# Layer-norm rows in two halves, with Newton roots on VectorE and the first row block loaded first

## The chip, the cores and the metric

The kernel runs on one core of one Trainium2 chip. The metric is the time of one execution on the device in microseconds (us). "Span" is the time from the first to the last instruction in a profiled execution; it is some 1.8 us shorter than the time of that same execution. Engines are named TensorE (PE in the profile, with PEld for its weight loads), VectorE (DVE), ScalarE (ACT), GpSimd (POOL) and SyncE (SP).

## The reference, cut to what matters

The result mixes two branches over the same rows x (2048 rows of 640). Branch A is a causal convolution over 2048 positions; branch B is a layer norm and an MLP that mixes positions.

```python
def _layernorm(x, axis=-1, eps=1e-5):
    m = jnp.mean(x, axis=axis, keepdims=True)
    v = jnp.var(x, axis=axis, keepdims=True)
    return (x - m) / jnp.sqrt(v + eps)

# branch A: S = 2048, D = 640
k_shift = sum over t of k_pad[:, t:t+S] * shift_k[:, 3-t]      # 4 filter taps   (paraphrased)
kv  = k_shift * v
y   = irfft(rfft(kv, 2*S) * rfft(ssm_k, 2*S))[:S] + kv * ssm_D #                 (paraphrased)
a   = q * y
# branch B: F = 1536
h = _layernorm(x, axis=-1)
u = _gelu(jnp.einsum("bsd,sf->bdf", h, w1) + b1)
b = (jnp.einsum("bdf,fs->bds", u, w2) + b2).transpose(0, 2, 1)

g = _sigmoid((x * gate_w).sum(-1, keepdims=True))              # x is also q
return g * a + (1 - g) * b
```

## The kernel before

The program builds a list of operations; a list scheduler then walks through a model of the engines (a duration and a priority for every operation) and fixes the order of instructions on each engine. So a changed duration in the model, or a changed operation, can move instructions anywhere. In the program that it hands over the order is fixed, with semaphores between the engines.

The work on TensorE is, in order: transposes of the filter `ssm_k`, two forward transforms of the filter (`wT` by the sine tables `FTB`), the tap convolution of k (`KF` by `KT`), the forward transforms of `kv` (`vkv`, `kv`), inverse transforms (by `GTB`), and in between the two MLP layers (`X` by `ring`, which holds w1; `GT` by `W`, which holds w2). MLP matmuls fill whatever holes the rest leaves, once rows of `X` are normalised.

The layer norm and the taps, before (the lines are those that the change touches):

```python
        def ln_tile(hk, p):                       # 16 row tiles of 128x640
            t = 4 * hk + p
            xs = X[:, hk, p, :]
            for ci in range(2):
                ... bn_stats(stats[:, t, 6*ci:6*ci+6], xs[:, 320*ci:320*ci+320])   # VectorE
            ... bn_aggr(mv[:, t, :], stats[:, t, :])                               # VectorE

        def ln_apply():
            ts("POOL", sd[:, :], mv[:, :, 1], 1e-5, None, ALU.add)
            tt("POOL", rstd[:, :], sd[:, :], V(cst, 1, [[0, 16]]), ALU.pow)        # power -0.5
            tt("POOL", sd[:, :], sd[:, :], rstd[:, :], ALU.mult)
            for t in range(16):
                xs = X[:, t // 4, t % 4, :]
                ts("DVE", xs, xs, mv[:, t, 0:1], rstd[:, t:t + 1], ALU.subtract, ALU.mult, ...)
        ...
                for hk in range(4):
                    for p in range(4):
                        ln_tile(hk, p)
                ln_apply()
                for g0 in (0, 10):                # filter taps spread out, two pieces of 128x2240
                    tt("POOL", KF[:, g0:g0 + 10, :, :], ..., ALU.mult)
                for hk in range(2):
                    k_turn(hk)                    # copies kp <- kn on VectorE, then a DMA transpose
                mixing(C[0], SS, 0, fine=True)    # sums and differences of the transformed filter, VectorE
```

The kv product, for which the first kv transform waits, is a VectorE operation behind all of these: `tt("DVE", o, kb[:, :, :], vi, ALU.mult, prio=0)`.

Of the kernel before, what the change touches and what calls it, by code (L numbers as in the profile page):

```python
# [11 lines left out]
I32 = mybir.dt.int32  # L12
# [296 lines left out]
class _Op:  # L309
    __slots__ = ("eng", "dur", "emit", "prio", "idx", "ndep", "succ", "vt", "vtrole", "end", "start", "kind", "lat", "deps", "name", "after", "nafter", "asucc")  # L310
# [12 lines left out]
class _Sched:  # L323
# [29 lines left out]
    def add(self, eng, dur, emit, reads, writes, prio=None, vt=None, lat=0.0, name=""):  # L353
# [4 lines left out]
        op.vt = vt  # L358
        deps = set()
# [22 lines left out]
    def run(self):  # L382
# [13 lines left out]
        free = {e: 0.0 for e in engs}  # L396
        dma_free = 0.0
# [14 lines left out]
        while started < n:  # L412
# [6 lines left out]
            for e in engs:  # L419
# [32 lines left out]
                if e in ("SP", "QA") or op.lat < 0:  # L452
                    issue = 0.1
                    s = max(t + issue, dma_free)
                    dma_free = s + op.dur
                    op.end = dma_free + 2.0 + (3.0 if e == "POOL" else 0.0)
                    free[e] = t + issue
                else:
                    op.end = t + op.dur
                    free[e] = op.end  # L460
# [44 lines left out]
def _build(nc, A_q, A_k, A_v, A_shift_k, A_ssm_k, A_ssm_D, B_x, B_w1, B_b1, B_w2, B_b2, gate_w, out):  # L505
# [10 lines left out]
    with ExitStack() as es:  # L516
# [97 lines left out]
        def tt(eng, o, a, b, op, mode=2, prio=None):  # L614
            n = n_of(o)
            d = dve_dur(n, mode) if eng == "DVE" else n / 500.0 + 0.3
            return SC.add(eng, d, lambda s: T.op(eng, lambda e: e.tensor_tensor(o, a, b, op), [a, b], [o]),  # L617
                          [a, b], [o], prio=prio, name="tt")

        def ts(eng, o, a, s1, s2, op0, op1=None, mode=1, prio=None, extra=0.0):  # L620
# [8 lines left out]
            return SC.add(eng, d, lambda s: T.op(eng, f, rr, [o]), rr, [o], prio=prio, name="ts")  # L629
# [90 lines left out]
        def k_turn(hk):  # L720
# [3 lines left out]
            SC.add("DVE", 0.75, lambda s: T.op("DVE", lambda e: e.tensor_copy(ov, iv), [i[:, :, :]], [o[:, :, :]]), [i[:, :, :]], [o[:, :, :]], prio=0, name="kperm")  # L724
# [13 lines left out]

        for hk in range(2):
            ssm_load(hk)  # L740
# [4 lines left out]
        x_load(0)  # L745
        dma(gwb[:, :], dr(gate_w, 0, [[0, 128], [1, D]]), 128 * 1280, chain=True)
        for hk in range(1, 4):
            x_load(hk)
        ssm_load(2)
        ssm_load(3)  # L750

# [3 lines left out]
        iota = lambda ap, pat, b, cm: SC.add("POOL", 0.5, lambda s: T.op("POOL", lambda e: e.iota(ap, pat, base=b, channel_multiplier=cm), [], [ap]), [], [ap])  # L755
# [20 lines left out]
        for hk in range(4):  # L776
            w1_load(0, hk)

# [43 lines left out]
        def mixing(R, Th, Ts, fine=False, conj=False):  # L822
# [26 lines left out]
        def ln_apply():  # L849
            ts("POOL", sd[:, :], mv[:, :, 1], 1e-5, None, ALU.add)  # L850
            tt("POOL", rstd[:, :], sd[:, :], V(cst, 1, [[0, 16]]), ALU.pow)
            tt("POOL", sd[:, :], sd[:, :], rstd[:, :], ALU.mult)
            for t in range(16):
                xs = X[:, t // 4, t % 4, :]
                ts("DVE", xs, xs, mv[:, t, 0:1], rstd[:, t:t + 1], ALU.subtract, ALU.mult, mode=4, extra=0.16)

        srcW = lambda h: (lambda kt, p, ci: wT[:, 2 * h + kt, p, 320 * ci:320 * ci + 320])
        for h in range(2):
# [5 lines left out]
            if h == 0:  # L864
                for hk in range(4):
                    for p in range(4):
                        ln_tile(hk, p)
                ln_apply()
                for g0 in (0, 10):
                    tt("POOL", KF[:, g0:g0 + 10, :, :], V(cw, 7 * g0, [[7, 10], [1, 7], [0, 32]]), V(m32, 0, [[0, 10], [0, 7], [1, 32]]), ALU.mult)  # L870
                for hk in range(2):
                    k_turn(hk)
                mixing(C[0], SS, 0, fine=True)
            else:
                mixing(C[1], C[0], 0, conj=True)
# [277 lines left out]
```

## Time and profile before

| | before |
|---|---|
| time, median of 3 (range) | 192.79 us (192.77 to 192.95) |
| span of the profiled execution, granted clock | 190.9 us, 1.0 |
| TensorE busy | 93% |
| chain of waits | TensorE 71%, VectorE 19% |

From the profile page of the kernel before: the head, the busy time of each engine, and the chain of work that ended last, by engine.

```profile
span 190.9 us, 3358 instructions
...
PE 177.4 (93%) x1403; PEld 130.5 (68%) x1403; DVE 170.3 (89%) x195; ACT 116.4 (61%) x187; POOL 33.0 (17%) x29
...
PE 71%; DVE 19%; DMA 4%; POOL 2%; issue 2%; SPq 0%; ACT 0%; DVEq 0%
```

TensorE is busy for most of the span, but the chain also runs through VectorE for 19% of it, so part of TensorE's time is set by VectorE. Where, the timeline shows. Its columns are: start in us, length in us, engine, line of the program, operation, output<-input, shapes, how many instructions are joined, and in brackets the idle time before it with what ended it. First TensorE before:

```profile
14.29 10.29 PE L293 MATMUL pp<-wT,FTB 128*128 128x320 bf16 x64 [0.43 <-ACT wT L655]
...
45.94 4.51 PE L293 MATMUL pp<-X,ring 128*128 128x320 bf16 x32
50.28 0.43 PE L293 MATMUL pp<-vkv,FTB 128*128 128x320 bf16 x2
51.75 3.75 PE L293 MATMUL pp<-vkv,FTB 128*128 128x320 bf16 x26 [1.04 <-DVE vkv L617]
55.34 1.25 PE L293 MATMUL pp<-X,ring 128*128 128x320 bf16 x8
...
72.09 4.01 PE L293 MATMUL pp<-kv,FTB 128*128 128x320 bf16 x28
...
83.10 34.93 PE L293 MATMUL pp<-X,ring 128*128 128x320 bf16 x256
117.87 32.76 PE L293 MATMUL pp<-GT,W 128*128 128x320 bf16 x240
...
180.02 7.77 PE L293 MATMUL pp<-GT,W 128*128 128x320 bf16 x56
```

Two matmuls of the kv transform start at 50.28, and the other 26 must wait for VectorE's product until 51.75. The group at 55.34, the MLP group right behind these 28 transform matmuls, is a good **checkpoint**: the waits for the layer norm and for the first kv product lie before it. From 117.87 the second MLP layer runs, and TensorE ends at 180.02 + 7.77 = 187.79.

VectorE before, around the root:

```profile
25.41 1.45 DVE L617 TENSOR_TENSOR C<-C 128x2560 bf16<-128x2560 bf16 x1
30.05 5.79 DVE L628 TENSOR_SCALAR X<-X,mv,rstd 128x640 bf16<-128x640 bf16 x16 [3.19 <-POOL rstd L617]
```

and GpSimd before, in the same stretch:

```profile
13.65 7.84 POOL L617 TENSOR_TENSOR KF<-cw,m 128x2240 bf16<-128x2240 bf16 x2 [5.40 <-DVE mv L847]
25.60 1.39 POOL L627 TENSOR_SCALAR sd<-mv 128x16 f32<-128x16 f32 x1 [4.11 <-DVE mv L847]
27.07 2.94 POOL L617 TENSOR_TENSOR rstd<-sd,cst 128x16 f32<-128x16 f32 x1
```

GpSimd's power on 128x16 values takes 2.94 us, and VectorE stands idle for 3.19 us until it is there. Only then, at 30.05, are rows scaled. The taps (`KF`, from 13.65 to 21.49) lie beside VectorE's row statistics, which are not slowed: one tile takes 0.85 to 0.86 us from start to start, ahead of the taps as beside them.

### The profile page before, as it was taken

To read this page: it belongs to the slowest core of one execution; us is meant where nothing else is said; L and a number is where in the kernel's file an instruction comes from. 1 tells how busy PE (TensorE), PEld (TensorE's weight loads), DVE (VectorE), ACT (ScalarE), POOL (GpSimd) and SP (SyncE) were. 2 spreads that over 40 slices of the span, in tenths; PEclk is the share of its full clock that TensorE was granted. 3 is DMA by queue.
4 is the path that set the end of the run, shared out by engine and by line. 5 is a ranking of instruction groups with operands and counts; after the bars stand their busy time and mean duration, and the time that the engine had idled before them with its cause. 6 is when DMAs were issued, how large, how long until landed. Compare 5 with 4: busy or idle time off the path is not lost.

```text
span 190.9 us, 3358 instructions
## 1 busy us (share of the span) xinstructions
PE 177.4 (93%) x1403; PEld 130.5 (68%) x1403; DVE 170.3 (89%) x195; ACT 116.4 (61%) x187; POOL 33.0 (17%) x29
## 2 busy tenths in 40 slices
PE   0749989999799999999999999999999999999993
PEld 0536555678566976767777777888888777886782
DVE  7999967999999799999999969999999958999451
ACT  4799997889599999998411221131322467516632
POOL 2619563600006300010012102250000000000000
PEclk9999999999999999999999999999999999999999
DMA  5999999993799999994368914999947903210222
GB/s 155 327 412 378 372 238 230 307 407 136 136 181 306 250 232 306 272 329 96 59 138 251 231 27 138 272 208 195 263 136 224 367 18 137 72 69 2 72 103 103
DMA packets 37296, 38.93 MB, mean 204 GB/s; under 512 B 15644, under 2 KB 32673, under 8 KB 37281
## 3 DMA queue, kind: packets, MB, share of 16 engines
q1 hardware_dynamic: 34464, 32.15, 54.7%
q0 software_dynamic: 2752, 6.55, 18.6%
q8 instruction: 11, 0.18, 0.4%
q14 instruction: 5, 0.03, 0.0%
q10 hardware_dynamic: 64, 0.01, 0.0%
HBM read 25.87 MB, written 2.62 MB: 149 GB/s over the span
## 4 chain that ended last, share of the span: by engine, by line
PE 71%; DVE 19%; DMA 4%; POOL 2%; issue 2%; SPq 0%; ACT 0%; DVEq 0%
PE pp L293 71%; DVE stats L845 6%; DMA X<-in_A_q_dram 4%; DVE X L628 3%; DVE SS L617 3%; DVE C L617 2%; DVE kp L724 2%; POOL rstd L617 2%; DVE vkv L617 1%; DVE mv L847 1%; POOL sd L627 1%; SPq L267 0%; ACT O L655 0%; DVE O L617 0%; DVEq L187 0%
## 5 line engine op out<-in xcount | busy, mean ns | idle before, releaser
L293 PE MATMUL pp<-X,ring 128*128 128x320 bf16 x384 | 54.0, 299 | 0.1
L293 PE MATMUL pp<-GT,W 128*128 128x320 bf16 x384 | 52.8, 299 | 0.0
L617 DVE TENSOR_TENSOR C<-C 128x2560 bf16<-128x2560 bf16 (+1 forms) x28 | 48.9, 1769 | 1.2 <-ACT C L655 1.1
L293 PEld LDWEIGHTS pp<-GT,W 128*128 128x128 bf16 x384 | 43.5, 113 | 8.9 <-ACT cgb L655 0.2
L293 PEld LDWEIGHTS pp<-X,ring 128*128 128x128 bf16 x384 | 37.1, 98 | 15.4 <-DVE X L628 0.7
L655 ACT ACTIVATE C<-pp 128x640 bf16<-128x640 f32 x64 | 39.6, 741 | 4.4 <-PE pp L293 4.3
L655 ACT ACTIVATE O<-pp,c,omg 128x640 bf16<-128x640 f32 (+1 forms) x17 | 14.5, 853 | 32.9 <-PE pp L293 32.9
L655 ACT ACTIVATE GT<-pp,cc 128x640 bf16<-128x640 f32 x12 | 9.6, 797 | 22.1 <-PE pp L293 21.9
L617 DVE TENSOR_TENSOR tm<-C,C 128x2560 bf16<-128x2560 bf16 (+2 forms) x12 | 20.2, 1708 | 1.9 <-DMA C<-tm 1.9
L293 PE MATMUL pp<-wT,FTB 128*128 128x320 bf16 x128 | 19.6, 310 | 0.6 <-ACT wT L655 0.4
L655 ACT ACTIVATE cgb<-pp,gg 128x640 bf16<-128x640 f32 x16 | 12.7, 793 | 7.7 <-PE pp L293 7.7
L293 PEld LDWEIGHTS pp<-wT,FTB 128*128 128x128 bf16 x128 | 11.5, 101 | 8.0 <-ACT C L655 2.3
L617 DVE TENSOR_TENSOR C<-tm 128x2560 bf16<-128x2560 bf16 (+1 forms) x12 | 15.0, 1263 | 0.1
L293 PE MATMUL pp<-ident,ssm 128*128 128x128 bf16 x80 | 8.8, 265 | 6.6 <-DMA ssm<-in_A_ssm_k_dram 5.3
L262 POOL DMA_DIRECT2D C<-C x6 | 7.5, 1407 | 36.0 <-DVE C L617 36.0
L845 DVE BATCH_NORM_STATS2 stats<-X 128x6 f32<-128x320 bf16 x32 | 13.4, 463 | 0.3 <-DMA X<-in_A_q_dram 0.3
L293 PE MATMUL pp<-C,GTB 128*128 128x320 bf16 x96 | 13.6, 299 | 0.0
L293 PEld LDWEIGHTS pp<-ident,ssm 128*128 128x128 bf16 x80 | 6.3, 127 | 9.1 <-DMA ssm<-in_A_ssm_k_dram 5.3
L293 PEld LDWEIGHTS pp<-C,GTB 128*128 128x128 bf16 x96 | 9.0, 98 | 4.0 <-ACT O L655 0.2
L655 ACT ACTIVATE gq<-gq 128x640 bf16<-128x640 bf16 x16 | 11.8, 756 | 0.0
L617 DVE TENSOR_TENSOR tm<-C,SS 128x5120 bf16<-128x5120 bf16 x4 | 11.2, 2817 | 0.0
L655 ACT ACTIVATE wT<-pp 128x640 bf16<-128x640 f32 x16 | 10.1, 812 | 1.1 <-PE pp L293 1.1
(64 smaller groups left out, 177.2 us busy)
## 6 DMA issues: line engine op xcount, KB each, us to landing
ring<-in_B_w_dram SPq DMA_DIRECT2D x12, 512.0 KB, 10.3
W<-in_B_w_dram SPq DMA_DIRECT2D x8, 768.0 KB, 7.3
C<-C POOLq DMA_DIRECT2D x6, 640.0 KB, 10.5
ssm<-in_A_ssm_k_dram SPq DMA_DIRECT2D x4, 640.0 KB, 9.1
X<-in_A_q_dram SPq DMA_DIRECT2D x4, 640.0 KB, 9.5
kn<-in_A_k_dram SPq DMA_DIRECT2D x4, 640.0 KB, 9.2
out_dram<-O SPq DMA_DIRECT2D x7, 320.0 KB, 2.3
vkv<-in_A_v_dram SPq DMA_DIRECT2D x2, 640.0 KB, 4.7
```

Of the source, the lines that this page charges most:

```text
L262: ins = engobj.dma_start(out_ap, in_ap, accum_op=ALU.add, max_dma_last_dim=2560)
L293: ins = self.nc.tensor.matmul(ps_ap, lhsT=lhsT, rhs=rhs, start=start, stop=stop, skip_group_check=True)
L617: return SC.add(eng, d, lambda s: T.op(eng, lambda e: e.tensor_tensor(o, a, b, op), [a, b], [o]), [a, b], [o], prio=prio, name="tt")
L627: return e.tensor_scalar(o, a, s1, None, op0=op0)
L628: return e.tensor_scalar(o, a, s1, s2, op0=op0, op1=op1)
L655: return T.op("ACT", lambda e: e.activation(o, src, func, **kw), rr + [src], ww)
L724: SC.add("DVE", 0.75, lambda s: T.op("DVE", lambda e: e.tensor_copy(ov, iv), [i[:, :, :]], [o[:, :, :]]), [i[:, :, :]], [o[:, :, :]], prio ...
L845: SC.add("DVE", 0.38, (lambda o, i: lambda s: T.op("DVE", lambda e: e.bn_stats(o, i), [i], [o]))(o, i), [i], [o])
L847: SC.add("DVE", 0.12, (lambda o, i: lambda s: T.op("DVE", lambda e: e.bn_aggr(o, i), [i], [o]))(o, i), [i], [o])
```

## The change

The intent: take the root off GpSimd, where VectorE waits for it, and work in two halves of eight row tiles, so that MLP matmuls can fill TensorE's early holes; load the first row block ahead of the filter rows so that statistics can start earlier; cut the taps into four pieces; and let the scheduler's model count with VectorE and GpSimd holding each other up. The model calls that a lock, and so does this document, for no more than what the traces show: an operation lasts until about the end of an instruction of the other engine that lies beside it. In the profile of the kernel before, GpSimd's 128x16 add, begun at 25.60 beside VectorE's subtraction (25.41 to 26.86), lasted 1.39 us, to 26.99; its 128x16 product at 30.09 took 0.22 us. The diff, cut to its core:

```diff
 # 1. loads
+        x_load(0)
         for hk in range(2):
             ssm_load(hk)
-        x_load(0)
-        dma(gwb[:, :], ...)
-        for hk in range(1, 4):
-            x_load(hk)
+        x_load(1)
+        w1_load(0, 0)
         ssm_load(2)
         ssm_load(3)
+        x_load(2)
+        w1_load(0, 1)
+        x_load(3)
+        # k, the other w1 blocks and gwb are loaded behind these
 # 2. the root, now 13 small VectorE operations for the columns a to b
-        def ln_apply():
-            ts("POOL", sd[:, :], mv[:, :, 1], 1e-5, None, ALU.add)
-            tt("POOL", rstd[:, :], sd[:, :], V(cst, 1, [[0, 16]]), ALU.pow)
-            tt("POOL", sd[:, :], sd[:, :], rstd[:, :], ALU.mult)
+        def ln_scale(a, b):
+            v, y, z, m_ = sd[:, a:b], rstd[:, a:b], gth[:, a:b], mv[:, a:b, 1]
+            ...
+                op(tensor_scalar(v, m_, 1e-5, None, op0=ALU.add))
+                op(tensor_scalar(yi, vi, 1, None, op0=ALU.logical_shift_right))
+                op(tensor_scalar(yi, yi, -1.0, float(0x5F3759DF), op0=ALU.mult, op1=ALU.add))
+                for _ in range(3):
+                    op(scalar_tensor_tensor(z = (y * -0.5) * y))
+                    op(tensor_tensor(z = z * v))
+                    op(scalar_tensor_tensor(y = (z + 1.5) * y))
+                op(tensor_tensor(v = v * y))
 # 3. halves, and taps in four pieces of 128x1120
+        LNG = ((0, 8), (8, 16))
+        KFP = (0, 5, 10, 15)
-                ln_apply()
-                for g0 in (0, 10):
-                    tt("POOL", KF[:, g0:g0 + 10, :, :], ...)
+                for a, b in LNG:
+                    for t in range(a, b):
+                        ln_tile(t // 4, t % 4)
+                    ln_scale(a, b)
+                    ln_apply(a, b)
+                for g0 in KFP:
+                    tt("POOL", KF[:, g0:g0 + 20 // len(KFP), :, :], ...)
 # 4. the scheduler's model
-                    issue = 0.1
+                    issue = 1.2 if e == "POOL" else 0.1      # issue of a GpSimd DMA
+                    if op.lock:                              # in the model VectorE and GpSimd hold each other up
+                        op.end += max(port["POOL" if e == "DVE" else "DVE"] - t, 0.0)
+                        port[e] = op.end
+                    # the model's durations of GpSimd operations changed a little too
 # 5. part of the mixing gets priority MIXP = 330
```

The 1.2 us and the durations are numbers of the model. In the profile of the kernel before, GpSimd's DMA issues show 0.86 to 1.71 us each (median 1.31 of the six `C<-C`, 0.86 of the four `C<-tm`).

More of the change, by code (lines that the diff above doesn't have):

```diff
@@ L309 @@
 class _Op:
-    __slots__ = ("eng", "dur", "emit", "prio", "idx", "ndep", "succ", "vt", "vtrole", "end", "start", "kind", "lat", "deps", "name", "after", "nafter", "asucc")
+    __slots__ = ("eng", "dur", "emit", "prio", "idx", "ndep", "succ", "vt", "vtrole", "end", "start", "kind", "lat", "deps", "name", "after", "nafter", "asucc", "lock")
 class _VT:
@@ L358, in add @@
         op.vt = vt
+        op.lock = eng == "POOL"
         deps = set()
@@ L396, in run @@
         free = {e: 0.0 for e in engs}
+        port = {"DVE": 0.0, "POOL": 0.0}
         dma_free = 0.0
@@ L615, in tt @@
             n = n_of(o)
-            d = dve_dur(n, mode) if eng == "DVE" else n / 500.0 + 0.3
-            return SC.add(eng, d, lambda s: T.op(eng, lambda e: e.tensor_tensor(o, a, b, op), [a, b], [o]),
-                          [a, b], [o], prio=prio, name="tt")
+            d = dve_dur(n, mode) if eng == "DVE" else n / 600.0 + 0.17
+            o_ = SC.add(eng, d, lambda s: T.op(eng, lambda e: e.tensor_tensor(o, a, b, op), [a, b], [o]),
+                        [a, b], [o], prio=prio, name="tt")
+            o_.lock = True
+            return o_
+        tt_ = tt
         def ts(eng, o, a, s1, s2, op0, op1=None, mode=1, prio=None, extra=0.0):
@@ L628, in f @@
                 return e.tensor_scalar(o, a, s1, s2, op0=op0, op1=op1)
-            return SC.add(eng, d, lambda s: T.op(eng, f, rr, [o]), rr, [o], prio=prio, name="ts")
+            o_ = SC.add(eng, d, lambda s: T.op(eng, f, rr, [o]), rr, [o], prio=prio, name="ts")
+            o_.lock = eng == "POOL" or mode > 1
+            return o_
         def stt(eng, o, a, sc, b, op0, op1, acc=None, prio=None):
@@ L723, in k_turn @@
             iv = V(i, 0, [[32, NG], [D, 4], [1, 32]])
-            SC.add("DVE", 0.75, lambda s: T.op("DVE", lambda e: e.tensor_copy(ov, iv), [i[:, :, :]], [o[:, :, :]]), [i[:, :, :]], [o[:, :, :]], prio=0, name="kperm")
+            SC.add("DVE", 0.75, lambda s: T.op("DVE", lambda e: e.tensor_copy(ov, iv), [i[:, :, :]], [o[:, :, :]]), [i[:, :, :]], [o[:, :, :]], prio=0, name="kperm").lock = True
             c0 = 16 + 128 * (hk % 2)
@@ L744, in _build @@
         small(rows[0:12, 2, 0:128], dr(B_b1, 0, [[128, 12], [1, 128]]), 3072, "QA")
-        x_load(0)
-        dma(gwb[:, :], dr(gate_w, 0, [[0, 128], [1, D]]), 128 * 1280, chain=True)
-        for hk in range(1, 4):
-            x_load(hk)
+        x_load(1)
+        w1_load(0, 0)
         ssm_load(2)
         ssm_load(3)
+        x_load(2)
+        w1_load(0, 1)
+        x_load(3)
         T_PI = float(np.float32(math.pi * (1.0 - 1e-6)))
@@ L754, in _build @@
         memset("DVE", cst[:, 1:2], -0.5)
-        iota = lambda ap, pat, b, cm: SC.add("POOL", 0.5, lambda s: T.op("POOL", lambda e: e.iota(ap, pat, base=b, channel_multiplier=cm), [], [ap]), [], [ap])
+        iota = lambda ap, pat, b, cm: SC.add("POOL", 0.2, lambda s: T.op("POOL", lambda e: e.iota(ap, pat, base=b, channel_multiplier=cm), [], [ap]), [], [ap])
         iota(dif[:, :], [[1, 128]], 0, -1)
@@ L775, in _build @@
             k_load(hk)
-        for hk in range(4):
+        for hk in range(2, 4):
             w1_load(0, hk)
+        dma(gwb[:, :], dr(gate_w, 0, [[0, 128], [1, D]]), 128 * 1280, chain=True)
         vt = _VT("cv")
@@ L820, in fwd, with mixing, tt @@
                     act(o, two, ACT.Copy, vt=vt, name=name + "e", **kw)
-        def mixing(R, Th, Ts, fine=False, conj=False):
+        def mixing(R, Th, Ts, fine=False, conj=False, prio=None):
+            def tt(*a):
+                return tt_(*a, prio=prio)
             def sl(h, s, n=1):
@@ L847, in ln_tile, with emit, op, ln_apply @@
             SC.add("DVE", 0.12, (lambda o, i: lambda s: T.op("DVE", lambda e: e.bn_aggr(o, i), [i], [o]))(o, i), [i], [o])
-        def ln_apply():
-            ts("POOL", sd[:, :], mv[:, :, 1], 1e-5, None, ALU.add)
-            tt("POOL", rstd[:, :], sd[:, :], V(cst, 1, [[0, 16]]), ALU.pow)
-            tt("POOL", sd[:, :], sd[:, :], rstd[:, :], ALU.mult)
-            for t in range(16):
+        def ln_scale(a, b):
+            v, y, z, m_ = sd[:, a:b], rstd[:, a:b], gth[:, a:b], mv[:, a:b, 1]
+            yi = y.bitcast(I32)
+            vi = v.bitcast(I32)
+            def emit(s):
+                def op(fn, rr, w):
+                    T.op("DVE", fn, rr, [w])
+                op(lambda e: e.tensor_scalar(v, m_, 1e-5, None, op0=ALU.add), [m_], v)
+                op(lambda e: e.tensor_scalar(yi, vi, 1, None, op0=ALU.logical_shift_right), [vi], yi)
+                op(lambda e: e.tensor_scalar(yi, yi, -1.0, float(0x5F3759DF), op0=ALU.mult, op1=ALU.add), [yi], yi)
+                for _ in range(3):
+                    op(lambda e: e.scalar_tensor_tensor(out=z, in0=y, scalar=-0.5, in1=y, op0=ALU.mult, op1=ALU.mult), [y], z)
+                    op(lambda e: e.tensor_tensor(z, z, v, ALU.mult), [z, v], z)
+                    op(lambda e: e.scalar_tensor_tensor(out=y, in0=z, scalar=1.5, in1=y, op0=ALU.add, op1=ALU.mult), [z, y], y)
+                op(lambda e: e.tensor_tensor(v, v, y, ALU.mult), [v, y], v)
+            return SC.add("DVE", 1.5, emit, [m_], [v, y, z], prio=0, name="rstd")
+        def ln_apply(a, b):
+            for t in range(a, b):
                 xs = X[:, t // 4, t % 4, :]
-                ts("DVE", xs, xs, mv[:, t, 0:1], rstd[:, t:t + 1], ALU.subtract, ALU.mult, mode=4, extra=0.16)
+                ts("DVE", xs, xs, mv[:, t, 0:1], rstd[:, t:t + 1], ALU.subtract, ALU.mult, mode=4, extra=0.16, prio=1)
+        MIXP = 330
+        LNG = ((0, 8), (8, 16))
+        KFP = (0, 5, 10, 15)
         srcW = lambda h: (lambda kt, p, ci: wT[:, 2 * h + kt, p, 320 * ci:320 * ci + 320])
@@ L864, in _build @@
             if h == 0:
-                for hk in range(4):
-                    for p in range(4):
-                        ln_tile(hk, p)
-                ln_apply()
-                for g0 in (0, 10):
-                    tt("POOL", KF[:, g0:g0 + 10, :, :], V(cw, 7 * g0, [[7, 10], [1, 7], [0, 32]]), V(m32, 0, [[0, 10], [0, 7], [1, 32]]), ALU.mult)
+                for a, b in LNG:
+                    for t in range(a, b):
+                        ln_tile(t // 4, t % 4)
+                    ln_scale(a, b)
+                    ln_apply(a, b)
+                for g0 in KFP:
+                    tt("POOL", KF[:, g0:g0 + 20 // len(KFP), :, :], V(cw, 7 * g0, [[7, 20 // len(KFP)], [1, 7], [0, 32]]), V(m32, 0, [[0, 20 // len(KFP)], [0, 7], [1, 32]]), ALU.mult)
                 for hk in range(2):
                     k_turn(hk)
-                mixing(C[0], SS, 0, fine=True)
+                mixing(C[0], SS, 0, fine=True, prio=MIXP)
             else:
-                mixing(C[1], C[0], 0, conj=True)
+                mixing(C[1], C[0], 0, conj=True, prio=MIXP)
         memset("POOL", KT[0][:, :, 15:16], 0.0)
```

## The prediction

> **What bounds the kernel now.** The chain of waits: TensorE 71% of the 190.9 us span, VectorE 19%. By the timeline TensorE has no gap from 64.64 to 187.81 us: 928 recorded matmuls, 133 ns each, granted clock 1.00. Only what happens before 64 us can pay. There it idles 5.3 us for filter rows, 2.8 for ScalarE evacuations. From 14.3 to 24.6 us (64 matmuls, 160 ns each) and to 29.2 us ScalarE's evacuations set the pace; no MLP matmul fills the holes, as no row is normalised before 30 us. The last stall, 50.3 to 51.75 us: the first kv transform waits for VectorE's kv product. Behind that is a VectorE chain: row statistics 8.8 to 25.4, GpSimd's root (1.4 + 2.9 us; VectorE idles 3.2), 16 row scalings 30.05 to 35.84, 15.9 us of mixing, copies, products.
>
> **What the change does.**
> - The first row block leads the DMA queue. A 655 kB block takes about 1.7 us, so the first filter rows land near 7 instead of 5.3 us. I expect no loss: ScalarE idled 1.1 us just then, and a sine moves there; the first transform still starts at 14.3 to 14.7.
> - GpSimd's root goes; two chains of 13 tiny VectorE operations come. The profile shows 0.17 to 0.23 us for 128x16 operations: estimated 1.7 to 2.6 us per chain, 3.4 to 5 in all, against 3.2 idle removed.
> - Half the rows are ready near 20 us instead of 33. 16 MLP matmuls (2.1 us) move into the ScalarE-paced holes. The second filter transform then runs without MLP work at ScalarE's pace, 16 x 0.605 = 9.7 us, instead of 12.5 with 24 mixed in.
> - Part of the mixing is demoted behind the kv product: 6.9 us of VectorE work.
> - Four filter-tap pieces on GpSimd now overlap row scalings and copies. [...]GpSimd's 128x16 add took 1.39 us, ending with VectorE's subtraction beside it. I charge VectorE 2 us.
>
> **How much is on the critical path.** Both kernels do 56 MLP matmuls before the first kv transform. New: ScalarE ends the second filter transform near 40.3 (before 41.9), 80 short kv matmuls take 4.3 us, 40 MLP matmuls 5.3: kv transform from 49.8, or about 50.5 if VectorE's products are late. Before, it truly ran from 51.75. Gain 1.2 to 2.0 us. From there TensorE binds both; the gain reaches the end unless the late order returns it: the inverse transforms come some 80 matmuls later in TensorE's order, leaving 12 MLP matmuls behind the last instead of 56. That costs 0 to 0.8 us.
>
> **Predicted:** 191.1 us, 8 in 10 between 189.2 and 192.9. Faster by over 2% 0.10, within 2% 0.87, slower 0.03.
>
> **What would show it.** First row scaling at 17 to 19 us; no GpSimd pow; 8 MLP matmuls before 26 us; second filter transform ending near 40 us; under 0.7 us of VectorE wait before the first kv transform, which starts near 50; TensorE gapless afterwards at 133 ns; TensorE's idle less by 1 to 2 us.
>
> **What would make it wrong.** Late filter rows delaying ScalarE's chain; a root chain over 3 us; [...]the second half of the rows later than 44 us; k loads, behind two weight blocks, delaying the kv transposes past 40 us; VectorE late for the inverse.

The terms behind 191.1 us: the kv transform from 49.8 to 50.5 us where it had run from 51.75, a gain of 1.2 to 2.0 us, less 0 to 0.8 us for the late order. Taken from 192.79 us that comes to 190.8 to 192.4 us, and 191.1 was set within it. The 2 us charged to VectorE stay, as the author's estimate; they do not follow from the one measured number beside them, the add of 1.39 us. The 1.7 us for a 655 kB block are an estimate, and the kernel before bears it out: the first filter rows were used from 5.34 us and the row block queued two places behind them from 8.77 us, 3.43 us for two blocks.

## The result and the profile after

| | before | after |
|---|---|---|
| time, median of 4 runs each (range) | 192.78 us (192.67 to 192.95) | 193.36 us (193.35 to 193.37) |
| ratio of fast runs, 95% interval | | 1.0029 (1.0012 to 1.0046) |
| span, granted clock | 190.9 us, 1.0 | 191.6 us, 1.0 |
| checkpoint (the MLP group behind 28 kv-transform matmuls) | 55.34 us | 55.12 us |
| from the checkpoint to the end of the span | 135.56 us | 136.48 us |

A ratio is the mean time of one kernel's fast runs over the mean of the other's fast runs of the same rounds, so it is not quite the ratio of the medians quoted beside it. The change is slower by about 0.6 us, and the prediction's range, 189.2 to 192.9 us, does not hold 193.36.

From the profile page of the kernel after, the lines that answer to those above:

```profile
span 191.6 us, 3381 instructions
...
PE 177.6 (93%) x1403; PEld 130.0 (68%) x1403; DVE 179.6 (94%) x221; ACT 116.3 (61%) x187; POOL 26.8 (14%) x28
...
PE 58%; DVE 29%; ACT 10%; issue 1%; POOL 0%; DVEq 0%; POOLq 0%
```

VectorE's busy time rose by 9.3 us (170.3 to 179.6) and its share of the chain from 19% to 29%. Twenty-six tiny operations should not take 9 us: at the 0.17 to 0.23 us that the 128x16 operations of the kernel before show, an estimate is 4.4 to 6.0 us. The timeline of VectorE after shows where it went (6.0 us are in three operations):

```profile
15.49 2.06 DVE L874 TENSOR_SCALAR sd<-mv 128x8 f32<-128x8 f32 x1
17.58 1.99 DVE L875 TENSOR_SCALAR rstd<-sd 128x8 int32<-128x8 int32 x1
19.61 1.99 DVE L876 TENSOR_SCALAR rstd<-rstd 128x8 int32<-128x8 int32 x1
21.63 0.17 DVE L878 SCALAR_TENSOR_TENSOR gth<-rstd 128x8 f32<-128x8 f32 x1
...
23.43 0.17 DVE L881 TENSOR_TENSOR sd<-sd,rstd 128x8 f32<-128x8 f32 x1
23.52 2.94 DVE L637 TENSOR_SCALAR X<-X,mv,rstd 128x640 bf16<-128x640 bf16 x8
...
37.56 0.17 DVE L874 TENSOR_SCALAR sd<-mv 128x8 f32<-128x8 f32 x1
...
39.98 0.17 DVE L881 TENSOR_TENSOR sd<-sd,rstd 128x8 f32<-128x8 f32 x1
40.07 1.49 DVE L622 TENSOR_TENSOR SS<-C 128x2560 bf16<-128x2560 bf16 x1
```

and the timeline of GpSimd after:

```profile
13.43 8.14 POOL L622 TENSOR_TENSOR KF<-cw,m 128x1120 bf16<-128x1120 bf16 x4 [5.15 <-ACT cw L666]
```

Counted to the start of the next operation, the same 13 operations took 8.0 us in the first chain (15.49 to 23.52) and 2.5 us in the second (37.56 to 40.07). In the second each takes 0.17 us, and they start 0.20 us apart. In the first, three operations on eight values per partition show 2.06, 1.99 and 1.99 us. Four tap pieces of 2.06 us each run on GpSimd from 13.43 to 21.57, and the three long operations end with the second, third and fourth piece. The rows are then scaled from 23.52; a chain of 2.5 us would have let them start near 18.0.

TensorE after:

```profile
14.07 9.70 PE L293 MATMUL pp<-wT,FTB 128*128 128x320 bf16 x60 [0.43 <-ACT wT L666]
...
44.39 5.60 PE L293 MATMUL pp<-X,ring 128*128 128x320 bf16 x40
49.82 0.43 PE L293 MATMUL pp<-vkv,FTB 128*128 128x320 bf16 x2
51.54 3.75 PE L293 MATMUL pp<-vkv,FTB 128*128 128x320 bf16 x26 [1.28 <-DVE vkv L622]
55.12 1.25 PE L293 MATMUL pp<-X,ring 128*128 128x320 bf16 x8
...
70.78 1.79 PE L293 MATMUL pp<-kv,FTB 128*128 128x320 bf16 x12
72.90 1.31 PE L293 MATMUL pp<-kv,FTB 128*128 128x320 bf16 x8 [0.32 <-ACT C L666]
...
82.20 36.02 PE L293 MATMUL pp<-X,ring 128*128 128x320 bf16 x264
118.06 43.63 PE L293 MATMUL pp<-GT,W 128*128 128x320 bf16 x320
...
186.59 1.79 PE L293 MATMUL pp<-GT,W 128*128 128x320 bf16 x12
```

TensorE is now ready for the kv transform earlier (49.82, before 50.28), but the wait for VectorE's product is longer (1.28, before 1.04), and the checkpoint came only 0.22 us sooner. Behind it time was lost:

- checkpoint: 55.12 - 55.34 = -0.22 us;
- from there to the second MLP layer: 118.06 - 55.12 = 62.94 us, before 117.87 - 55.34 = 62.53 us, so +0.41 us;
- from there to TensorE's end: 188.38 - 118.06 = 70.32 us, before 187.79 - 117.87 = 69.92 us, so +0.40 us;
- from TensorE's end to the end of the span: 3.22 us, before 3.11 us, so +0.11 us.

The sum is +0.70 us, the difference of the spans (which the profile gives to 0.1 us only). So there are two questions: who took the gain ahead of the checkpoint, and what costs 0.9 us behind it.

The second item of this list can be placed: all of it lies in the second kv transform. Its 64 matmuls, with 16 MLP matmuls among them, took 11.42 us (70.78 to 82.20), before 11.01 us (72.09 to 83.10). The stretches ahead of it and behind it are equal, once the eight MLP matmuls that moved from ahead of it to behind it are allowed for (1.09 us).

### The profile page after: what moved, and what is told of

It reads as the page before. It is cut to its first block, busy times and chain, and to the rows that moved or that the text cites. A ratio compares the mean times of both kernels' runs of the same rounds, so it can differ in the third digit from the quotient of the medians.

```text
span 191.6 us, 3381 instructions
## 1 busy us (share of the span) xinstructions
PE 177.6 (93%) x1403; PEld 130.0 (68%) x1403; DVE 179.6 (94%) x221; ACT 116.3 (61%) x187; POOL 26.8 (14%) x28
## 4 chain that ended last, share of the span: by engine, by line
PE 58%; DVE 29%; ACT 10%; issue 1%; POOL 0%; DVEq 0%; POOLq 0%
PE pp L293 58%; DVE stats L862 6%; ACT C L666 3%; DVE C L622 3%; DVE SS L622 3%; DVE X L637 3%; ACT ksh L666 2%; ACT gq L666 2%; DVE pint L636 2%; DVE kp L735 2%; DVE vkv L622 1%; DVE pint L622 1%; ACT cgb L666 1%; DVE rstd L875 1%; DVE rstd L876 1%
## 5 line engine op out<-in xcount | busy, mean ns | idle before, releaser
L293 PE MATMUL pp<-wT,FTB 128*128 128x320 bf16 x128 | 20.1, 311 | 0.6 <-ACT wT L666 0.4
L293 PEld LDWEIGHTS pp<-wT,FTB 128*128 128x128 bf16 x128 | 10.8, 101 | 9.4 <-ACT C L666 4.4
L293 PE MATMUL pp<-C,GTB 128*128 128x320 bf16 x96 | 14.1, 299 | 0.0
L293 PE MATMUL pp<-ident,ssm 128*128 128x128 bf16 x80 | 8.0, 265 | 4.0 <-DMA ssm<-in_A_ssm_k_dram 3.4
L293 PE MATMUL pp<-vkv,FTB 128*128 128x320 bf16 x64 | 9.5, 300 | 1.3 <-DVE vkv L622 1.3
```

Of the source, the lines that this page charges most:

```text
L293: ins = self.nc.tensor.matmul(ps_ap, lhsT=lhsT, rhs=rhs, start=start, stop=stop, skip_group_check=True)
```

## The experiments

The main theory: the tap pieces on GpSimd hold up VectorE's first root chain, that delays the row scalings and everything behind them on VectorE, and the kv transform waits for it. Rivals: the Newton chain itself is too long; the new load order delays the front; the halves are of no use; the scheduler's new order costs the time, whatever the lock does.

In most experiments the scheduler's order was left alone and single operations were replaced or moved after it had run, so that nothing else moves. That the orders agree was verified by comparing the instruction order of each engine.

### kf_late: the taps out of the way

The changed kernel, with every order kept, except that the four tap pieces wait until VectorE has done both first copies of k.

```diff
+        # after the scheduler has run
+        turn = [o for o in SC.order if o.name == "kperm"][1]
+        # take the four tap operations out, put them behind `turn`, and let each wait
+        # for the count that VectorE has reached there
+        T.do_waits("POOL", {"DVE": kf_at[0]})
```

> The changed kernel with every engine's order kept, only the four filter-tap pieces on GpSimd are held until VectorE has done its second k copy. Theory ([...]GpSimd's tap pieces hold VectorE's first root chain, 15.5 to 23.5 us): the first chain falls from 8.0 to about 2.6 us, the first row scaling moves from 23.5 to about 18.1, the second kv product ends near 47 to 49.8 instead of 51.5, TensorE's 1.28 us wait before the first kv transform goes, and the time falls by 1.0 to 1.3 us, to 192.1 to 192.4. Rival 1 (13 dependent operations, a first use of integer operations or the read of fresh statistics are slow in themselves): the chain still takes over 6 us, time 193.3. Rival 2 (whatever the front gains is given back, since the later order is what binds): the wait goes but the time stays within 0.3 us of 193.36.

Measured: 192.00 us (191.80 to 192.41, 5 runs), ratio to before 0.9959 (0.9947 to 0.9972); 1.36 us under the changed kernel and a little better than expected. Its VectorE timeline:

```profile
15.48 0.17 DVE L874 TENSOR_SCALAR sd<-mv 128x8 f32<-128x8 f32 x1
15.69 0.17 DVE L875 TENSOR_SCALAR rstd<-sd 128x8 int32<-128x8 int32 x1
...
17.99 2.93 DVE L637 TENSOR_SCALAR X<-X,mv,rstd 128x640 bf16<-128x640 bf16 x8
...
33.03 3.23 DVE L622 TENSOR_TENSOR C<-C 128x2560 bf16<-128x2560 bf16 x1
```

its GpSimd timeline:

```profile
25.51 9.40 POOL L622 TENSOR_TENSOR KF<-cw,m 128x1120 bf16<-128x1120 bf16 x4 [17.23 <-DVE kp L735]
```

and its TensorE timeline:

```profile
49.67 4.30 PE L293 MATMUL pp<-vkv,FTB 128*128 128x320 bf16 x28
53.81 1.25 PE L293 MATMUL pp<-X,ring 128*128 128x320 bf16 x8
```

The chain now takes 2.5 us (15.48 to 17.99), the rows are scaled 5.5 us earlier, no wait for VectorE is reported before the kv transform (the 28 matmuls take 4.30 us, against 4.01 in one_group_again below, so some 0.3 us of it may be hidden inside), and the checkpoint falls at 53.81: 1.31 us before the changed kernel's. Behind the checkpoint nothing changed: 190.3 - 53.81 = 136.49 us, against 136.48. So the pieces' old place cost 1.3 us of the time. A data dependency does not explain the slow chain: here the chain ended at 17.99, long before the first piece started at 25.51. Of the 5.5 us that the chain gained, most did not arrive. VectorE then stood idle for 1.69 us, for a k load. And the lock is not free even here: the pieces now lie beside VectorE's statistics and mixing from 25.5 to 34.9, and two operations of the mixing on 128x2560 took 2.10 and 3.23 us, where 1.49 us each is usual in the changed kernel.

### kf_fine: taps in twenty pieces, left where they were

If a VectorE operation waits for a whole GpSimd instruction, shorter instructions should make shorter waits, and more of them. The orders are kept; each tap piece is cut into five.

```diff
-  tt("POOL", KF[:, g0:g0+5], ...)                     # 128x1120
+  for g in range(g0, g0 + 5):
+      T.op("POOL", tensor_tensor(KF[:, g:g+1], ...))  # 128x224
```

> The changed kernel with every order kept, each of the four tap pieces cut in five (20 GpSimd instructions of 128x224). Theory (each VectorE root operation[...] waits for one GpSimd instruction[...]): short pieces do not help as long as there are more pieces left than root operations: about 15 pieces of 0.4 to 0.6 us are left when the chain starts, so each of the 13 operations waits for one, the chain takes 6 to 8.5 us again and the time stays at 193.2 to 193.6. Rival (it is the length of one piece that hurts[...]): the chain falls under 4.5 us and the time to 192.2 to 192.6.

Measured: 192.64 us (192.63 to 192.92, 4 runs), ratio 0.9996 (0.9981 to 1.0011). The chain took 6.3 us, as the theory said, but the time is a miss: it fell, where 193.2 to 193.6 us had been expected. Its VectorE and GpSimd timelines:

```profile
16.13 0.48 DVE L876 TENSOR_SCALAR rstd<-rstd 128x8 int32<-128x8 int32 x1
...
21.32 0.48 DVE L881 TENSOR_TENSOR sd<-sd,rstd 128x8 f32<-128x8 f32 x1
21.73 3.99 DVE L637 TENSOR_SCALAR X<-X,mv,rstd 128x640 bf16<-128x640 bf16 x8
```

```profile
13.43 10.68 POOL L911 TENSOR_TENSOR KF<-cw,m 128x224 bf16<-128x224 bf16 x20 [5.16 <-ACT cw L666]
```

From the third on, every operation of the chain takes 0.48 or 0.49 us, one for each tap piece (10.68 / 20 = 0.53 us a piece, and the operations start 0.52 us apart). In this chain the two engines take turns, one instruction each. This is the clearest evidence of the lock: what a held operation shows goes with the length of GpSimd's instruction (0.48 us beside pieces of 0.53 us, 1.99 to 2.06 us beside pieces of 2.06 us), and the operation is the same. The chain lasts 6.3 us instead of 8.0, and the eight scalings 3.99 instead of 2.94. The checkpoint is at 54.37, 0.75 us earlier than after, and the time fell by as much (0.72 us).

### newton_only: the new root alone, in the old kernel

The kernel before with all its orders; GpSimd's three root operations are dropped and the 13 VectorE operations put there, over all 16 columns at once.

```diff
-            ts("POOL", sd, mv[:, :, 1], 1e-5, None, ALU.add)
-            tt("POOL", rstd, sd, ..., ALU.pow)
-            tt("POOL", sd, sd, rstd, ALU.mult)
+            # 13 VectorE operations over 16 columns, as in the change
```

> The kernel before with every engine's order kept; only GpSimd's three root operations are replaced by one chain of 13 VectorE operations over all 16 columns, at the same place, when no tap piece runs. Theory: the chain takes about 2.6 us (25.5 to 28.1), row scalings start near 28.1 instead of 30.05, the second kv product ends 1.9 us earlier (near 49.8), TensorE's 1.04 us wait at 51 goes and the time falls 1.0 to 1.5 us, to 191.3 to 191.8. Rival (the chain costs VectorE as much as GpSimd's root in any place): 192.5 to 193.

Measured: 192.08 us (192.01 to 192.16, 5 runs), ratio 0.9963 (0.9950 to 0.9975). Faster than before by 0.7 us, but short of what was expected. Its VectorE timeline:

```profile
25.54 1.44 DVE L617 TENSOR_TENSOR C<-C 128x2560 bf16<-128x2560 bf16 x1
26.89 0.17 DVE L859 TENSOR_SCALAR sd<-mv 128x16 f32<-128x16 f32 x1
...
29.50 5.79 DVE L628 TENSOR_SCALAR X<-X,mv,rstd 128x640 bf16<-128x640 bf16 x16
```

The chain takes 2.6 us here (26.89 to 29.50), hardly more for 16 columns than for 8, so it was not too long by itself. But the scalings start only 0.55 us sooner than before (29.50 against 30.05). Before, VectorE was idle for 3.19 us, yet it had done the 1.45 us difference while GpSimd worked; now chain and difference stand in one line. What the chip gives back is the idle time (3.19) less the chain (2.61). The checkpoint, 54.79, is 0.55 us earlier, and the rest is the same as before: 190.4 - 54.79 = 135.61 us.

### old_loads and x_second: the load order

First the load order alone was undone in the changed kernel.

```diff
-        x_load(0)
         for hk in range(2): ssm_load(hk)
-        x_load(1); w1_load(0, 0); ssm_load(2); ssm_load(3); x_load(2); w1_load(0, 1); x_load(3)
+        x_load(0); dma(gwb, ...); x_load(1); x_load(2); x_load(3); ssm_load(2); ssm_load(3)
```

> The load order undone (first filter rows first, all row blocks, then filter rows, k, weights), the rest of the change kept. The first row block then lands near 8.8 instead of below 8 us, so the first chain starts some 0.5 us later and still meets three or four tap pieces. Theory (the load order is not what costs): the first chain still takes 7 to 8 us, and the time is 193.0 to 193.7. Rival (rows first delays the filter, and that is the loss): 192.5 or less.

Measured: 192.27 us (192.18 to 193.16, 4 runs), ratio 0.9982 (0.9966 to 0.9998). This is below the 193.0 to 193.7 us expected and in the rival's range. But it does not settle it, as the scheduler found another order too. The first root chain is still held (it lasts 6.7 us, 16.73 to 23.42), but the stretch behind the checkpoint is 190.4 - 54.89 = 135.5 us, 1.0 us shorter than after. So a second run kept every order and moved one queue entry only: the first row block goes behind the first two filter blocks.

```diff
+        sp = [o for o in SC.order if o.eng == "SP"]
+        SC.order.remove(sp[0])
+        SC.order.insert(SC.order.index(sp[2]) + 1, sp[0])
```

> The changed kernel, all orders kept, only the first row block queued behind the first two filter row blocks, so that the load order alone is tested (old_loads also changed the schedule). Theory (the load order neither costs nor gains: the first transform is paced by ScalarE's sines and evacuations, and the first chain ends when the tap pieces end): first filter rows land near 5.3 instead of 7 us, first row statistics near 8.8 instead of 8.2, the first row scaling stays at 23.4 to 23.7, time 193.2 to 193.6. Rival (rows first delays the filter path and that is part of the loss): 192.9 or less.

Measured: 193.37 us (193.35 to 193.39, 4 runs), ratio 1.0029 (1.0014 to 1.0043), the same as the changed kernel. The first filter matmul starts at 5.41 instead of 7.06 us, and the filter transform still at 14.06 (after: 14.07); the first row scaling is at 23.52 in both. Loading rows first is neutral here. The first operation of the root chain shows why:

```profile
16.08 1.45 DVE L874 TENSOR_SCALAR sd<-mv 128x8 f32<-128x8 f32 x1
```

It started 0.59 us later than after (15.49) and was held 0.61 us less (1.45 against 2.06 us), to the end of the same tap piece. So the pieces, and not the load, set when the rows are scaled. What the load order is worth with the pieces out of the way was not tested.

### tail_issue and late_tail: the end of the kernel

The changed kernel leaves 12 MLP matmuls behind the last inverse transform, the kernel before 56. Part of that comes from the model's longer issue time for GpSimd DMAs. One number back:

```diff
-                    issue = 1.2 if e == "POOL" else 0.1
+                    issue = 0.1
```

> The changed kernel with one number of the scheduler's model put back (issue time of a GpSimd DMA 1.2 to 0.1 us); the orders differ from the changed kernel's only after 150 us: the last inverse transform has 24 MLP matmuls behind it instead of 12, and fewer are mixed in between the inverses. Theory (the tail's late, finely mixed inverse costs TensorE a wait of 0.36 us at 180 us and 0.1 us after its end): time falls 0.3 to 0.6 us, to 192.8 to 193.1. Rival (the tail's order costs nothing, the loss is all in front): 193.3 to 193.4.

Measured: 192.97 us (192.91 to 193.22, 5 runs), ratio 1.0011 (0.9998 to 1.0023), 0.39 us under after. The orders differ only beyond 150 us, with 24 MLP matmuls behind the last inverse. The stretch from the checkpoint to the end is 191.0 - 54.96 = 136.04 us, against 136.48. So about 0.4 us of the loss behind the checkpoint belongs to this number in the model. The small rest of the profiled difference lies ahead of the checkpoint (54.96, after 55.12), where the orders are the same. Both edits together:

```diff
+ (the edit of kf_late)
+ (the edit of tail_issue)
```

> Both repairs at once: tap pieces held until the second k copy (as in kf_late) and the tail order of tail_issue. Theory (two separate losses, [...]): they add, 191.5 to 191.8 us. Rival (the two share one cause, the late VectorE, so the second repair gives nothing once the first is in): 191.9 to 192.1.

Measured: 191.78 us (191.66 to 191.92, 5 runs), ratio 0.9948 (0.9936 to 0.9959). From the checkpoint on it needs 190.1 - 54.00 = 136.1 us, as tail_issue does. But 191.78 is only 0.22 us under kf_late, for its checkpoint, at 54.00 in this execution, is later than kf_late's 53.81 with the same order; more of that below, at late_gq.

### late_model: the old model, with the taps held back

Could the scheduler do without the lock in its model, once the taps are held behind the eighth row scaling?

```diff
-                    issue = 1.2 if e == "POOL" else 0.1
+                    issue = 0.1
-                    if op.lock:
+                    if False and op.lock:
-            d = ... if eng == "DVE" else n / 600.0 + 0.17
+            d = ... if eng == "DVE" else n / 500.0 + 0.3
+        # tap operations wait for the eighth row scaling
```

> The search for a better version: the changed kernel scheduled with the old model[...], which puts the first eight MLP matmuls after 32 of 64 transform matmuls and the inverses where the kernel before had them, with the tap pieces held until the eighth row scaling. Theory: ScalarE no longer idles 0.65 to 1.3 us before the last evacuation of the first filter transform, the first kv transform starts near 49 to 49.7 without a wait, the 0.3 us ScalarE wait near 72 us may go, and the tail is as cheap as before: 190.8 to 191.5 us. Rival (the old model places VectorE work that the pieces now hold up, or the rows are not ready at 19.4 us): 191.8 to 192.6.

Measured: 194.05 us (194.03 to 194.10, 5 runs), ratio 1.0064 (1.0051 to 1.0077): a miss. TensorE here waits 1.22 us for second-half rows and 0.79 us for the kv product, and has 72 MLP matmuls before the kv transform instead of 56. So going back to the old model, with the taps held, does not win the time back: the scheduler's order was worse. It is one trial, with the taps held at another place than in kf_late.

### one_group and one_group_again: no halves

One constant of the change is set back, so that all 16 tiles share one chain. The scheduler then finds its own order.

```diff
-        LNG = ((0, 8), (8, 16))
+        LNG = ((0, 16),)
```

> The halves undone: one Newton chain over 16 columns after all statistics, everything else of the change kept (the scheduler then also chooses a tail with 40 MLP matmuls behind the last inverse). Theory (the loss is the meeting of the first chain with the tap pieces; a single chain near 28 us comes when they are done at about 21.5): chain about 2.7 us, no wait or under 0.4 us before the first kv transform, 191.7 to 192.3 us. Rival (the halves are worth having even with the lock): 193.4 or more.

The first of its runs, the profiled one, was slow: 313.93 us at a granted clock of 0.578. The five fast runs were 191.25, 191.59, 191.96, 192.34 and 192.65 us, ratio 0.9956 (0.9936 to 0.9976).

> The same kernel as one_group, whose profile fell on an execution at a granted clock of 0.58. Expected again 191.3 to 192.6 us at full clock; in the profile a root chain of about 2.7 us after the tap pieces have ended, and no wait, or under 0.4 us, of TensorE for VectorE's products before the first kv transform. Rival: a chain over 5 us or a wait over 1 us.

Measured: 191.14 us (191.00 to 191.36, 4 runs), ratio 0.9914 (0.9901 to 0.9927), 2.2 us under the changed kernel; the five fast runs of one_group, of the same kernel in another round, have a median of 191.96 us, 1.4 us under it. Its VectorE and TensorE timelines:

```profile
30.61 0.16 DVE L874 TENSOR_SCALAR sd<-mv 128x16 f32<-128x16 f32 x1
...
33.10 0.18 DVE L881 TENSOR_TENSOR sd<-sd,rstd 128x16 f32<-128x16 f32 x1
```

```profile
48.68 4.01 PE L293 MATMUL pp<-vkv,FTB 128*128 128x320 bf16 x28
52.52 1.25 PE L293 MATMUL pp<-X,ring 128*128 128x320 bf16 x8
```

The taps are where they were after (13.42 to 21.55), but the root comes at 30.61, when they are long done, and takes 2.6 us. The halves are what put the first root chain beside the taps. The checkpoint is at 52.52 with 48 MLP matmuls before it instead of 56; eight take 1.09 us in the changed kernel (55.12 to 56.21), so it corresponds to 53.61, a little better even than kf_late's 53.81. So normalising half of the rows early, even when the lock is out of the way, gains nothing that this profile shows (between executions of one order this stretch differs by more than these 0.2 us; see late_gq): TensorE before 42 us goes largely at ScalarE's pace (in this profile the chain that ended last lies on ScalarE's evacuations from 15.35 to 28.64 us; in the changed kernel the sixteen evacuations of the second filter transform, 0.605 us apart, follow each other without a gap from 31.55 to 41.27 us), and it is enough that rows are ready for the matmuls behind. The stretch to the end, 189.2 - 53.61 = 135.6 us, is also that of the kernel before; the 0.9 us loss is not there.

### late_gq and best: looking for a faster kernel

In after, kf_late and late_tail TensorE waits 0.32 to 0.33 us for ScalarE near 72 us. In late_gq one gate sum on ScalarE comes two evacuations later, on top of late_tail.

```diff
+        # on top of late_tail: ScalarE's sixth gate sum, two evacuations later
+        SC.order.remove(acts[k_])
+        SC.order.insert(SC.order.index(acts[k_ + 2]) + 1, acts[k_])
```

> late_tail with one ScalarE operation moved: the gate sum that stands between the MLP evacuation and the next transform evacuations near 71.5 us goes two evacuations later; every other order is kept. Theory (it is this operation that makes TensorE wait 0.33 us for ScalarE near 71.8 us, which the kernel before did not): the wait goes, the time falls from 191.78 by 0.2 to 0.35 us, to 191.4 to 191.6. Rival (TensorE's wait only moves to a later place): 191.7 to 191.9.

Measured: 192.07 us (191.62 to 192.17, 5 runs), ratio 0.9955 (0.9943 to 0.9967), against 0.9948 for late_tail: no gain. The wait is gone as a line, but from the checkpoint to the second MLP layer it is 62.92 us (54.30 to 117.22), as in late_tail (54.00 to 116.94, 62.94). The second kv transform took 11.40 us (69.96 to 81.36), as long as after. A wait removed at one place came back in the pace of the next matmuls.

The two profiles show one more thing. Their orders are the same up to that gate sum, yet the 60 matmuls of the first filter transform, which start within 0.01 us of each other, took 9.55 us in late_gq and 10.71 us in late_tail: from 15.6 to 18.6 us late_tail did 17 of these matmuls and late_gq 27. In kf_late's profile a granted clock of 0.50 stands beside this slow pace (14.6 to 16.6 us, 10 matmuls); in late_tail's the clock reads 1.00 (10 matmuls in the same stretch). This is a difference between executions, not between kernels, and it bounds what can be told apart here. It does not all reach the end: in late_gq's profile VectorE waited 0.47 us for a k load and brought the kv product so late that TensorE waited 1.27 us for it, and the checkpoint (54.30) came after late_tail's (54.00).

Last, a kernel that combines all that helped: late_gq's edits, twenty tap pieces held only until the eighth row scaling, and the first two MLP groups moved in among the filter transposes.

```diff
+  # late_gq, and:
+  # taps: 20 pieces of 128x224, held until the eighth row scaling
+  # the first two MLP groups placed behind the 2nd and 6th of the second half's filter transposes
```

> late_gq, and: tap pieces of 128x224 held only until the eighth row scaling; the first two MLP groups of eight matmuls moved from in front of the last four filter matmuls into the transposes behind them. Theory: ScalarE no longer idles 0.65 us before the last evacuation of the first filter transform, so everything it paces up to the kv matmuls comes 0.6 us earlier; VectorE loses under 0.5 us to the short pieces instead of 2.4 us; the first kv transform starts near 49 to 49.5: 190.7 to 191.2 us. Rival (VectorE's second kv product, not ScalarE, then binds near 50 us): 191.3 to 191.6.

Measured: 191.44 us (191.06 to 191.85, 6 runs), ratio 0.9931 (0.9920 to 0.9943), above the 190.7 to 191.2 expected and in the rival's range. It beats both kernels, and so does one_group_again with one line of edit. The nine fast runs of one_group and one_group_again together average 191.60 us, so the order of these two and of late_tail (191.78) is not settled.

### All of it in one table

The checkpoint and the rest, from the one profiled execution of each kernel. As the two filter transforms of late_gq and late_tail show, small differences between checkpoints are not differences between kernels. Where the number of MLP matmuls ahead of the checkpoint is not 56, the checkpoint is corrected by 0.136 us for each (1.09 us for eight).

| kernel | time, median us | checkpoint | from checkpoint to end |
|---|---|---|---|
| before | 192.78 | 55.34 | 135.6 |
| newton_only | 192.08 | 54.79 | 135.6 |
| one_group_again | 191.14 | 53.61 (52.52 + 1.09) | 135.6 |
| old_loads | 192.27 | 54.89 | 135.5 |
| after | 193.36 | 55.12 | 136.5 |
| x_second | 193.37 | 55.12 | 136.5 |
| kf_fine | 192.64 | 54.37 | 136.4 |
| kf_late | 192.00 | 53.81 | 136.5 |
| tail_issue | 192.97 | 54.96 | 136.0 |
| late_tail | 191.78 | 54.00 | 136.1 |
| late_gq | 192.07 | 54.30 | 136.0 |
| best | 191.44 | 53.70 | 136.1 |
| late_model | 194.05 | 56.15 (58.33 - 2.18) | 136.1 |

The last column takes only three values (to 0.1 us), each given by the order of instructions; the lock moves only the checkpoint.

## Why the prediction was wrong, point by point

**What bounds the kernel: right for the gain.** It was to come ahead of about 64 us, and the kv transform's wait for VectorE was the place: in kf_late, kf_fine and newton_only the time fell with the checkpoint. But orders behind 64 us could lose time: old_loads and tail_issue got most of theirs back there (1.0 and 0.4 us).

**Loads: right.** Filter rows were expected near 7 us and without loss. They were used from 7.06 us, the first transform started at 14.07 (expected 14.3 to 14.7), and x_second shows the order to be neutral while the tap pieces stand where they do.

**The root chain: right by itself, wrong in place.** 1.7 to 2.6 us were estimated for 13 operations; alone they took 2.5 to 2.6 us in all kernels. The first chain of the changed kernel took 8.0 us.

**The step that failed: "Four filter-tap pieces on GpSimd now overlap row scalings and copies ... I charge VectorE 2 us."** That the two engines hold each other up was foreseen, and traces agree: a 128x8 operation of 0.17 us took 2.06 us beside a 2.06 us tap piece; 0.48 us beside pieces of 0.53 us. By what means was not shown; the 2 us was the estimate. Its size was off: the lock cost the first chain 8.0 - 2.5 = 5.5 us, not 2. The pieces started at 15.46, 17.48 and 19.51, each 0.03 to 0.10 us ahead of the operation that it held. So here the cost had to be counted as the number of GpSimd pieces that meet VectorE operations, times a piece's whole length (three times 2.06 us, less the 0.5 us that the three operations need: 5.7), and not as a share of the work. The pieces also did not meet scalings and copies, as the prediction had it, but the root chain, where every operation needs the one before it and nothing else can fill the gap. The prediction's list of what would make it wrong held both signs, "a root chain over 3 us" and VectorE held for over 4 us; they came as 8.0 and 5.5 us. The row statistics had not been hindered by taps in the kernel before, where they kept their 0.85 to 0.86 us for each tile, and that made the taps look harmless. Why the statistics are not held and the operations of the chain are was not shown.

**So the dependent expectations fell.** First row scaling at 17 to 19 us: measured 23.52, and 17.99 with the taps held. Eight MLP matmuls before 26 us: the eight started at 24.11, so that one held, barely. Wait ahead of the kv transform under 0.7 us: measured 1.28, and none in kf_late. A gain of 1.2 to 2.0 us ahead of the kv transform: measured 0.22 at the checkpoint, 1.53 (55.34 - 53.81) in kf_late, inside the range. With the lock out of the way the time is 192.00 us, inside the predicted range of 189.2 to 192.9, halfway between the predicted 191.1 and its end. So of the 2.26 us between 191.1 and 193.36 some 1.4 are missing ahead of the checkpoint (0.22 in place of 1.2 to 2.0), 1.3 of them through the lock, and 0.9 were lost behind it.

**Second filter transform at ScalarE's pace: right.** It was to take 9.7 us and to end near 40 us; it took 9.67 us from 30.58. ScalarE's evacuations ended at 41.27, though, 1 us later than the 40.3 from which the prediction counted on; the kv matmuls started at 40.22 without waiting for them, so that the start of the kv transform (49.8 predicted, TensorE ready at 49.82) came out right partly by luck.

**"The late order costs 0 to 0.8 us": right for the tail, short for the whole.** From the second MLP layer to the end 0.51 us were lost (0.40 + 0.11), of which tail_issue gives back about 0.4. The other 0.41 us, between the checkpoint and the second MLP layer, was not foreseen: the prediction had TensorE gapless at 133 ns there. A wait of 0.32 us for ScalarE is visible, but late_gq removed it and gained nothing. old_loads and one_group, which the scheduler ordered otherwise in this stretch, do not lose it. So it comes with the order of instructions there, in the second kv transform (11.42 us, against 11.01 before and 10.91 in one_group_again). In the kernel before, ScalarE stands idle for 0.35 us before its first evacuation of this transform (at 72.84); in the changed kernel it comes straight from a gate sum (at 72.11). That points to ScalarE's work just ahead, but it was not tested beyond late_gq, and the cause stays open.

**Demoting the mixing: right in effect, not by the new priority.** Part of the mixing does lie behind the first kv product in the changed kernel. But built without the new priority the orders are the same, so this came from the other parts of the change.

**Halves: wrong as a reason for the gain.** The prediction drew its gain from half of the rows being ready early. With one group the checkpoint is no later, and the taps are no longer in the way.

## What to carry to other kernels

Before moving a chain of small dependent operations to VectorE, look at what GpSimd runs in that window. Here each held operation lasted about as long as one whole GpSimd instruction, so three tiny operations beside 2.06 us pieces took 6.0 us. What helped was to move either of the two in time (a chain of 2.5 us in kf_late, of 2.6 us in one_group_again, after 8.0), and less so to cut GpSimd's instructions short (6.3 us in kf_fine). In newton_only removing a wait was worth the idle time less the work that took its place on the waiting engine (3.19 less 2.61 us, and the scalings came 0.55 us sooner), not the length of the removed operations (1.39 and 2.94 us). And where a scheduler fixes the orders, split the time at a checkpoint and keep the orders fixed in experiments: the gain ahead of it and the loss behind it were two causes, which one total had hidden.

## What the traces show of held operations, and of one slow run

- A chain on VectorE and a row of instructions on GpSimd took turns, one instruction each: 13 dependent VectorE operations took 8.0 us beside three pieces of 2.06 us (three operations held), 6.3 us beside pieces of 0.53 us (twelve held, at 0.41 to 0.49 us, the first not), 2.5 us alone (kf_late).
- An operation held this way is shown as busy, not as idle. No wait was reported before the three held operations, and their 2.06, 1.99 and 1.99 us, with 0.17 us each when not held, are 5.5 of the 9.3 us by which VectorE's busy time rose.
- One link in a chain of such small dependent operations took 0.20 us from start to start at 8 columns (kf_late) and 0.21 us at 16 (newton_only), of which the operation itself shows 0.17 us.
- A power on GpSimd on 128x16 fp32 values took 2.94 us, more than the 13 VectorE operations that replaced it (2.6 us).
- The first filter transform took 9.55 and 10.71 us in two kernels with the same order there; the difference is 0.6% of the span. kf_late's profile shows a granted clock of 0.50 at the slow pace, late_tail's 1.00 at the same pace; the cause was not shown. In the slow run of one_group the granted clock lay between 0.5 and 0.6 in every slice of its page from 15.6 us to the end, with TensorE busy for 96% of the span; a 128x320 matmul of the first MLP layer showed 438 ns on the mean, against 299 ns in one_group_again, and the run took 313.93 us where the others of the same kernel took 191.25 to 192.65.
